# A list scheduler's cost table is lengthened, its integer additions move from VectorE to GpSimd, and the last output rows get buffers of their own

## The chip, the core and the metric

The kernel runs on one core of a Trainium2 chip. A core has a matrix engine (TensorE, "PE" in the profile; its weight loads are the row "PEld"), three engines that work elementwise (VectorE "DVE", ScalarE "ACT", GpSimd "POOL"), and a queue engine (SyncE "SP") that issues every transfer here. Each engine runs its own instruction list strictly in order and waits for the others by semaphores. The metric is device time in microseconds (us) of one execution; lower is better.

## The reference

Three layers follow each other: block-causal attention, a three-way maximum layer, and a squared-ReLU layer.

```python
scores = (1 / np.sqrt(64)) * np.matmul(q, k.transpose(0, 1, 3, 2))      # q, k, v: (4, 8, 576, 64)
scores = np.where(block_i >= block_j, scores, -1e9)                     # blocks of 64 rows
scores = scores - np.max(scores, axis=-1, keepdims=True)
attn = np.exp(scores)
attn = attn / (np.sum(attn, axis=-1, keepdims=True) + 1e-09)
x = np.matmul(attn, v).transpose(0, 2, 1, 3).reshape(2304, 512)
y = np.maximum(np.maximum(x @ w1, x @ w2), x @ w3) @ moe_w_out          # 512 -> 768 -> 512
h = np.maximum(y @ w_in, 0.0)                                           # 512 -> 2048
out = (h * h) @ w_out                                                   # 2048 -> 512
```

All is float32. The weights arrive as 64-bit numbers, which the kernel turns into float32 itself.

## The kernel before, in words

**Precision.** Most products are made of three matmuls: an operand is split into a rounded part and the rest ("h" and "l" tiles such as `w1h`, `w1l`, `xh`, `xl`), and low times high, high times low and high times high are added in PSUM.

**Stages.** In the first stage (0 to about 370 us) 16 pairs of heads go through attention (`attn_pair`) while the first dense layer (`mlp1`, PSUM tiles `l`) of the batches already done fills the gaps on PE. A pair runs through `step(i)` for i = 0 to 3 and `last_step`: score matmuls (`sc`), the masked corner written by a memset, the row maximum by a reduction on DVE (`nm`, negated), a small multiplication of `nm` by the scale 0.125, the exponential on ACT (`P`, which also applies the scale to the scores), transposes on PE (`tp`), copies of them on ACT (`ta`, `tb`), and the value matmuls (`av`). Pairs 0 to 3 use plain float32 scores; for pairs 4 to 15 `score_operands` rounds `qs`, `kh` and forms the rests. From about 370 to 510 us PE does the rest of `mlp1` alone, while DVE, ACT and POOL prepare the second layer's weights in eight rounds (`second_rows`, `first_rows`, tiles `wqf`, `wq`). From about 510 us the second dense pair runs as 3 passes of 8 blocks (`up`, `down`; PSUM tiles `ph`, `acc`), 24 blocks in all.

**Weight chunks.** `load_w_` turns one chunk of 128x512 64-bit numbers into float32 by integer work: two ACT instructions read the high and low halves, DVE shifts, DVE merges the sign (scalar_tensor_tensor), and an integer addition joins the two; then ACT rounds the high part and DVE forms the rest. There are 18 chunks of `w1`, 6 of `wo1` and 16 of `wo2` (tiles `wos`, started behind the 56th mark of attention) whose addition runs on DVE; the profile shows it as `CUSTOM_DVE_ANT_0`, the order as `ISA`. The 16 chunks of the second layer (`wi`) already add on GpSimd.

**What sets the order.** A list scheduler (`Plan`) records every operation with its operands, and `issue` then places them one by one: among all operations whose inputs are known it takes, for the engine that can begin earliest, the one with the lowest rank (attention 0, the first layer 1, `wo2` chunks 2). It reckons with the times of `duration`, with `SEM` (the delay from one engine to another), `LAP` (overlap of neighbours on one engine), with `transfer` for DMAs and with `HOLD` for the port that DVE and POOL share in its model. The order it finds is final: on the chip each engine follows it, whatever the real times are. Operations given to `nc.any` go to ACT or DVE as the plan finds it sooner.

**The last rows.** `down` ends a pass by copying six accumulators of 128x512 (1_0, 1_1, 1_2, 0_0, 0_1, 0_2 in this order) into `ob` tiles, by turns on ACT and DVE, and sending them out. All `ob` tiles share two buffers (tag `wraw`).

Of the kernel before, what the change touches and what calls it, by code (L numbers as in the profile page):

```python
# [43 lines left out]

CFG = dict(PD=-1, PE=1, A1=0, A2=0, WP=1, FC=(8, 16), WO=55, FI=0, LO2=0, HI2=0, Q2=0, RN=3, XL=2, HL=2, SO=0, TF=0, W_A=0.7, W_B=1.5, SPARE='hl..rhl..rhl..r..r..r', S=15, PB=3, QB=(2, 2, 3), BANKS=(3, 2, 1, 2), LO=0, HI=0, Q=0, EV=('a', 'a'), EV2=('a', 'a'), CB=2, PC=0, PM=1000, PX=-0.5, PO=0, HH='*', XH='*', N0='a', YS='a', HIS=0, RB=1, TB=(2, 1), KB=1, CT='a', LT='d', XA=4, XB=0)
W_A, W_B = CFG["W_A"], CFG["W_B"]
# [4 lines left out]
PB = CFG["PB"]  # L51
MASKED = -1000000000.0 / SCALE

# [115 lines left out]
class Plan:  # L169
# [56 lines left out]
    def issue(self):  # L226
# [11 lines left out]
        def offer(op):  # L238
            for e in op.engines:
                when = 0.0  # L240
                for d in op.deps:
                    when = max(when, d.end + (SEM[d.engine] if d.engine != e else 0))
                waiting[e][op.index] = when, shares_port(e, op)
# [4 lines left out]
        for _ in ops:  # L248
# [12 lines left out]
            op.engine = e  # L261
            length = duration(e, op)
            if e in held and waiting[e][i][1]:
# [26 lines left out]

HOLD = dict(dve=120, pool=60)


# [52 lines left out]
def fused_kernel(ctx: ExitStack, tc: tile.TileContext, z0, k0, qk, v, w123, wo1, win2, wo2, out):  # L346
# [6 lines left out]
    ident.tile.make()  # L353
    ident.tile.constant = True
    make_identity(tc.nc, ident.tile.real)
    dram = Pool(nc, dram)
# [17 lines left out]

    def load_w_(src, hi, lo, name, f=None, adder=nc.vector):
        spare = SPARE[len(chunks)] if len(chunks) < len(SPARE) else "."
# [25 lines left out]
        if not CFG["HIS"]:  # L402
            adder.tensor_tensor(out=fi, in0=fi, in1=qi, op=ALU.add)
        if hi is None:
# [44 lines left out]
    def score_operands(n):  # L449
# [3 lines left out]
        for h in range(2):  # L453
            raw = at.tile([128, 2, S], F32, tag="raw", bufs=CFG["RB"], name=f"raw{n}_{h}")
            nc.sync.dma_start(out=raw, in_=qk[n, :, h])
            qs, kh, kl = [at.tile([128, S], F32R, tag=t, bufs=m, name=f"{t}_{n}_{h}")
                          for t, m in zip(("qs", "kh", "kl"), CFG["QB"])]
            nc.scalar.copy(out=qs, in_=raw[:, 0])
            nc.scalar.copy(out=kh, in_=raw[:, 1])
            nc.vector.tensor_tensor(out=qs[64:128], in0=raw[64:128, 0], in1=qs[64:128].bitcast(F32), op=ALU.subtract)  # L460
            nc.vector.tensor_tensor(out=kl, in0=raw[:, 1], in1=kh.bitcast(F32), op=ALU.subtract)
            score.append([(qs, kh), (qs, kl)])
# [54 lines left out]
    def attn_pair(n, groups=(0, 1)):  # L517
# [29 lines left out]
        def step(i):  # L547
# [6 lines left out]
            if share:  # L554
                both = sc[0][:, :2 * N].rearrange("p (h k) -> p h k", h=2)
                sc = [both[:, h] for h in range(2)]
                P = [P[0][:, N * h:N * h + N] for h in range(2)]
            nm = small(f"nm{name}")
            sm = sums[i // 2][:, 2 * (i % 2):2 * (i % 2) + 2] if direct else small(f"sm{name}")
            for h in range(2):  # L560
                for c, (qp, kp) in enumerate(score[h]):
                    mm(sc[h][:, :N], qp[:, 128 * i - q0:128 * i - q0 + 128], kp[:, :N], start=c == 0,
                       stop=c == len(score[h]) - 1)
                if not share:
                    nc.vector.memset(sc[h][0:64, N - 64:N], MASKED)
                    nc.vector.tensor_reduce(out=nm[:, h:h + 1], in_=sc[h][:, :N], axis=AX.X, op=ALU.max, negate=True)
            if share:
                nc.vector.memset(both[0:64, :, N - 64:N], MASKED)
                nc.vector.tensor_reduce(out=nm, in_=both, axis=AX.X, op=ALU.max, negate=True)
            nc.vector.tensor_scalar(out=nm, in0=nm, scalar1=SCALE, scalar2=None, op0=ALU.mult)  # L570
            for h in range(2):
                act = nc.scalar.activation(out=P[h][:, :N], in_=sc[h][:, :N], func=AF.Exp, bias=nm[:, h:h + 1],
                                           scale=SCALE, accum_out=sm[:, h:h + 1])
            if not direct:
# [222 lines left out]
    def second_rows(q):  # L797
        f = forms_f[q] = w2p.tile([128, 8, 256], F32, tag="wqf", name=f"wqf{q}")
        load_w_(win2[q + NQ], None, None, f"wi_{q + NQ}", f[:, 0:2].rearrange("p i n -> p (i n)"), nc.gpsimd)

    def first_rows(q):
        f, w = forms_f[q], wq_tile(q)
        load_w_(win2[q], None, None, f"wi_{q}", f[:, 2:4].rearrange("p i n -> p (i n)"), nc.gpsimd)
        a21, a22, a11, a12, s1, s2, s3, s4 = [f[:, i] for i in range(8)]
# [132 lines left out]
    def down(p, q):  # L937

        for m, h in ((0, 0), (1, 1), (0, 1), (1, 0)):
            gh, gl = g_t.pop((p, q, m, h))  # L940
            hi, lo = wo_t[p, q + NQ * m]
            for s in range(TH // 128):
# [6 lines left out]
                if last:  # L949
                    ob = m1.tile([128, DM], F32, tag="wraw", bufs=2, name=f"ob{p}_{h}_{s}")  # L950
                    if s % 2:
                        nc.vector.tensor_copy(out=ob, in_=a)
                    else:
                        nc.scalar.copy(out=ob, in_=a)
                    t0 = 2 * TH * p + TH * h + 128 * s
                    nc.sync.dma_start(out=out[t0:t0 + 128, :], in_=ob)
                yield
# [77 lines left out]
```

## Time and profile before

| what | value |
|---|---|
| median of 3 runs | 896.17 us (895.51 to 896.87) |
| the profiled execution | 894.74 us |
| its span, first to last instruction | 893.0 us |
| PE busy, share of the span | 97% |
| DVE busy | 69% |
| ACT busy | 48% |
| POOL busy | 6% |
| share of PE in the chain that ended last | 88% |

The profiled execution is 1.4 us under the median, and its span 1.7 us under its own time. Busy times of PE are modelled at their ends, so a stretch in which PE shows no gap may still have room; gaps that are shown are real. The rows further down name an instruction by engine, operation, output<-input and shape; in square brackets stands the idle time of the engine just before it and what ended that.

### The profile page before, as it was taken

The page shows a single profiled execution, that of the slowest core. Times are in us where ns is not written, and L with a number is a line of the kernel's source. Part 1 is how long each engine was busy: PE and PEld are TensorE (multiplying, and loading weights), DVE is VectorE, ACT ScalarE, POOL GpSimd, SP SyncE. Part 2 cuts the span into 40 slices and gives each one's busy share as a digit, 9 for nine tenths or more (in the row PEclk, how much of TensorE's full clock was granted, in tenths as well). Part 3 has the DMA queues.
Part 4 walks back from the last instruction along what each step waited for, and adds up shares of the span by engine and source line. Part 5 has one row for each costly group of instructions (what it writes and reads, how often), then busy time and mean ns, then how long its engine had stood idle before and what let it go on. Part 6 is the DMA issues. An engine that isn't in the chain of part 4 may idle for free.

```text
span 893.0 us, 14824 instructions
## 1 busy us (share of the span) xinstructions
PE 868.1 (97%) x5464; PEld 778.7 (87%) x5464; DVE 617.1 (69%) x1454; ACT 424.6 (48%) x1023; POOL 50.9 (6%) x54
## 2 busy tenths in 40 slices
PE   6889999999999999999999999999999999999997
PEld 4667888998899978999999998898988889889885
DVE  5799888878798969846667774547755457545542
ACT  6798777777688578525546321113311114211111
POOL 0000000000000000015453300000000000000000
PEclk9999999999999999999999999999999999999999
DMA  9545432233356564435668485464755546564211
GB/s 299 184 157 165 154 123 86 85 103 125 101 175 232 164 209 156 158 125 216 232 253 314 134 293 192 159 229 165 277 218 188 202 152 232 204 226 164 78 64 71
DMA packets 51912, 157.73 MB, mean 177 GB/s; under 512 B 8576, under 2 KB 15744, under 8 KB 48256
## 3 DMA queue, kind: packets, MB, share of 16 engines
q1 hardware_dynamic: 51840, 156.78, 50.4%
q8 instruction: 43, 0.70, 0.3%
q14 instruction: 29, 0.24, 0.1%
HBM read 124.26 MB, written 32.51 MB: 176 GB/s over the span
## 4 chain that ended last, share of the span: by engine, by line
PE 88%; DVE 5%; DMA 3%; ACT 3%; issue 1%; SPq 0%; ACTq 0%; DVEq 0%
PE l L187 30%; PE acc L187 22%; PE ph_x L187 11%; PE ph_y L187 8%; PE av L187 6%; PE sc L187 5%; PE tp L187 4%; DMA raw<-in_qk 2%; PE sc_t L187 1%; DVE nm L187 1%; PE tp_t L187 1%; DMA raw_wo<-in_wo 1%; PE r L187 1%; DMA out<-ob 0%; DVE P L187 0%
## 5 line engine op out<-in xcount | busy, mean ns | idle before, releaser
L187 PE MATMUL acc<-woh,g 128*128 128x512 f32 x576 | 200.4, 396 | 0.0
L187 PE MATMUL l<-xh,w1l 128*128 128x256 f32 (+1 forms) x576 | 174.0, 302 | 0.0
L187 PE MATMUL l<-xl,w1h 128*128 128x256 f32 (+1 forms) x576 | 173.1, 300 | 0.0
L187 PE MATMUL l<-xh,w1h 128*128 128x256 f32 (+1 forms) x576 | 172.8, 300 | 0.0
L187 ACT CAST g<-c 128x384 fp32r<-128x384 f32 x96 | 49.2, 513 | 239.3 <-DVE c L187 239.2
L187 PEld LDWEIGHTS acc<-woh,g 128*128 128x128 f32 x576 | 108.1, 188 | 20.5
L187 PEld LDWEIGHTS l<-xh,w1l 128*128 128x128 f32 x576 | 109.7, 190 | 3.4 <-issue 1.7
L187 PE MATMUL acc<-wol,g 128*128 128x512 f32 x288 | 112.0, 389 | 0.0
L187 PEld LDWEIGHTS l<-xl,w1h 128*128 128x128 f32 x576 | 109.6, 190 | 2.7 <-issue 1.9
L187 PEld LDWEIGHTS l<-xh,w1h 128*128 128x128 f32 x576 | 109.6, 190 | 1.6 <-issue 1.0
L187 PE MATMUL ph_x<-t,wq 128*128 128x384 f32 x432 | 87.6, 338 | 0.0
L187 DVE TENSOR_TENSOR g<-c,g 128x384 fp32r<-128x384 f32 x96 | 53.2, 556 | 44.7 <-ACT g L187 44.3
L187 PEld LDWEIGHTS ph_x<-t,wq 128*128 128x128 f32 x432 | 77.4, 188 | 5.8
L187 ACT ACTIVATE P<-sc,nm 128x128 f32<-128x128 f32 (+3 forms) x128 | 67.2, 531 | 13.0 <-DVE nm L187 10.6
L187 DVE TENSOR_TENSOR run<-l,run 128x256 f32<-128x256 f32 (+1 forms) x96 | 43.5, 453 | 32.4 <-PE l L187 27.7
L187 PE MATMUL tp<-ident,P 128*128 128x128 f32 x320 | 51.0, 282 | 10.6 <-ACT P L187 10.2
L187 PEld LDWEIGHTS acc<-wol,g 128*128 128x128 f32 x288 | 54.2, 188 | 7.2
L187 PE MATMUL ph_y<-b,wq 128*128 128x384 f32 x288 | 58.4, 337 | 0.0
L187 PE MATMUL l<-hh,wo1l 128*128 128x256 f32 (+1 forms) x192 | 56.9, 299 | 1.4 <-DVE hh L187 1.3
L187 PE MATMUL l<-hl,wo1h 128*128 128x256 f32 (+1 forms) x192 | 57.1, 300 | 0.0
L187 PE MATMUL l<-hh,wo1h 128*128 128x256 f32 (+1 forms) x192 | 56.8, 298 | 0.0
L187 DVE TENSOR_REDUCE nm<-sc 128x2 f32<-128x256 f32 (+2 forms) x96 | 55.7, 591 | 0.8
(132 smaller groups left out, 1561.2 us busy)
## 6 DMA issues: line engine op xcount, KB each, us to landing
wq<-wq_d SPq DMA_DIRECT2D x20, 1792.0 KB, 8.2
wq_d<-wq SPq DMA_DIRECT2D x8, 1792.0 KB, 5.9
raw<-in_qk SPq DMA_DIRECT2D x24, 576.0 KB, 3.9
wol<-wo_d SPq DMA_DIRECT2D x48, 256.0 KB, 3.3
woh<-wo_d SPq DMA_DIRECT2D x48, 256.0 KB, 4.0
raw_wo<-in_wo SPq DMA_DIRECT2D x22, 512.0 KB, 3.6
raw_w<-in_w SPq DMA_DIRECT2D x18, 512.0 KB, 5.0
wo_d<-wos SPq DMA_DIRECT2D x16, 512.0 KB, 3.2
```

The lines of the kernel that those rows point to most:

```text
L187: return getattr(engine, op_name)(*map(value, args), **{k: value(x) for k, x in kw.items()})
```

## The change

- `issue` adds 500 ns to the moment from which PE may use what another engine made, and multiplies every DVE and ACT duration by 1.07 (`SLOW`).
- The integer addition of all chunks is recorded on GpSimd.
- `EV`: the copies `ta` go to `nc.any`, so the plan chooses ACT or DVE.
- For pairs 4 to 15 the scale 0.125 is applied when `qs` is rounded; the multiplication of `nm` is left out in their four steps (48 of 64).
- A small exponential on a new tile `warm` stands at the start.
- In the last pass the four last `ob` tiles get buffers that the first layer's weights had (`w1h0`, `w1l0`, `w1h1`, `w1l1`), chosen by (3h + s) modulo 4, and the last rows (0_2) are copied and sent in two halves.

```diff
@@ issue
-                    when = max(when, d.end + (SEM[d.engine] if d.engine != e else 0))
+                    when = max(when, d.end + ((SEM[d.engine] + (500 if e == 'pe' else 0)) if d.engine != e else 0))
...
-            length = duration(e, op)
+            length = duration(e, op) * SLOW[e]
...
+SLOW = dict(pe=1, dve=1.07, act=1.07, pool=1, sp=1)
@@ CFG
-EV=('a', 'a')
+EV=('*', '*')
@@ fused_kernel
+    warm = const.tile([128, 1], F32, name="warm")
+    tc.nc.vector.memset(warm, 0.0)
+    tc.nc.scalar.activation(out=warm, in_=warm, func=AF.Exp)
@@ load_w_
-            adder.tensor_tensor(out=fi, in0=fi, in1=qi, op=ALU.add)
+            nc.gpsimd.tensor_tensor(out=fi, in0=fi, in1=qi, op=ALU.add)
@@ score_operands
-            nc.scalar.copy(out=qs, in_=raw[:, 0])
+            nc.scalar.activation(out=qs, in_=raw[:, 0], func=AF.Copy, scale=SCALE)
...
-            nc.vector.tensor_tensor(out=qs[64:128], in0=raw[64:128, 0], in1=qs[64:128].bitcast(F32), op=ALU.subtract)
+            nc.vector.scalar_tensor_tensor(out=qs[64:128], in0=raw[64:128, 0], scalar=SCALE,
+                                           in1=qs[64:128].bitcast(F32), op0=ALU.mult, op1=ALU.subtract)
@@ step
+            scale = SCALE if sf else 1.0
...
-            nc.vector.tensor_scalar(out=nm, in0=nm, scalar1=SCALE, scalar2=None, op0=ALU.mult)
+            if sf:
+                nc.vector.tensor_scalar(out=nm, in0=nm, scalar1=SCALE, scalar2=None, op0=ALU.mult)
...
-                                           scale=SCALE, accum_out=sm[:, h:h + 1])
+                                           scale=scale, accum_out=sm[:, h:h + 1])
@@ down
-                    ob = m1.tile([128, DM], F32, tag="wraw", bufs=2, name=f"ob{p}_{h}_{s}")
-                    if s % 2:
-                        nc.vector.tensor_copy(out=ob, in_=a)
+                    if p + 1 == NPASS and (h, s) not in ((1, 0), (1, 1)):
+                        home = ("w1h0", "w1l0", "w1h1", "w1l1")[(3 * h + s) % 4]
+                        ob = w1p.tile([128, DM], F32, tag=home, name=f"ob{p}_{h}_{s}")
                     else:
-                        nc.scalar.copy(out=ob, in_=a)
+                        ob = m1.tile([128, DM], F32, tag="wraw", bufs=2, name=f"ob{p}_{h}_{s}")
                     t0 = 2 * TH * p + TH * h + 128 * s
-                    nc.sync.dma_start(out=out[t0:t0 + 128, :], in_=ob)
+                    parts = 2 if p + 1 == NPASS and (h, s) == (0, TH // 128 - 1) else 1
+                    for i in range(parts):
+                        n = slice(DM // parts * i, DM // parts * (i + 1))
+                        cp("d" if (s + i) % 2 else "a", out=ob[:, n], in_=a[:, n])
+                        nc.sync.dma_start(out=out[t0:t0 + 128, n], in_=ob[:, n])
```

The order changes nearly everywhere in the first stage. Three places matter for what follows. The first is the start of ACT's list: `P0_0_0` is the exponential of pair 0, step 0; `raw_w1_0_0` the first weight chunk. Before:

```order
L187 ACT_TABLE_LOAD
L187 ACTIVATE P0_0_0_127,sm0_0_128<-sc0_0_0_117,nm0_0_123 128x128 x2
L187 ACTIVATE raw_w1_0_0_83<-raw_w1_0_0_83 128x512
L187 COPY ta0_143<-tp0_0_0_138 128x2x128
L187 ACTIVATE P0_1_0_148,sm0_0_128<-sc0_1_0_120,nm0_1_135 128x256 x2
```

Now:

```order
L360 ACT_TABLE_LOAD
L360 ACTIVATE warm_61<-warm_61 128x1
L187 ACTIVATE raw_w1_0_0_86<-raw_w1_0_0_86 128x512
L187 ACTIVATE P0_0_0_138,sm0_0_139<-sc0_0_0_120,nm0_0_127 128x128 x2
L187 ACTIVATE P0_1_0_149,sm0_0_139<-sc0_1_0_122,nm0_1_135 128x256 x2
```

The table load and the small exponential stand ahead, the chunk has moved in front of the first exponential of the scores, and the copy of the first transposes has left the list.

The second is DVE around step 3 of pair 1: `sc1_3_0` and `sc1_3_1` are the scores of its two heads, `nm1_3` the maxima that its exponentials wait for, `w1l3` and `raw_w1_3_x` chunk work. Before:

```order
L187 ISA f_w1_3_0_594<-raw_w1_3_0_316,f_w1_3_0_594 128x1024
L187 SCALAR_TENSOR_TENSOR raw_w1_3_1_499<-raw_w1_3_1_499 128x512
L187 TENSOR_TENSOR xl0_1_677<-av0_1_586,xh0_1_663 128x320
L187 ISA raw_w1_3_1_499<-raw_w1_3_1_499 128x1024
L187 TENSOR_TENSOR w1l3_692<-f_w1_3_0_594,w1h3_675 128x512
L187 MEMSET sc1_3_0_564 64x64
L187 MEMSET sc1_3_1_650 64x64
L187 TENSOR_SCALAR raw_w1_3_2_579<-raw_w1_3_2_579 128x512
L187 TENSOR_REDUCE nm1_3_706<-sc1_3_0_564 128x1
L187 TENSOR_TENSOR w1l3_692<-raw_w1_3_1_499,w1h3_675 128x512
L187 TENSOR_REDUCE nm1_3_706<-sc1_3_1_650 128x1
```

Now:

```order
L187 MEMSET sc1_3_0_562 64x64
L187 SCALAR_TENSOR_TENSOR f_w1_3_0_551<-raw_w1_3_0_348,f_w1_3_0_551 128x512
L187 TENSOR_TENSOR run0_0_0_2_592<-l1_0_0_0_2_544,run0_0_0_1_534 128x256
L187 TENSOR_REDUCE nm1_3_596<-sc1_3_0_562 128x1
L187 TENSOR_TENSOR w1l2_526<-f_w1_2_2_488,w1h2_509 128x512
L187 TENSOR_SCALAR raw_w1_3_1_478<-raw_w1_3_1_478 128x512
L187 TENSOR_TENSOR w1l3_631<-f_w1_3_0_551,w1h3_617 128x512
L187 TENSOR_TENSOR av0_1_586<-av0_1_586,rs0_1_627 128x320
L187 SCALAR_TENSOR_TENSOR raw_w1_3_1_478<-raw_w1_3_1_478 128x512
L187 MEMSET sc1_3_1_629 64x64
L187 TENSOR_REDUCE nm1_t_652<-sc1_t0_637 128x1
L187 TENSOR_REDUCE nm1_3_596<-sc1_3_1_629 128x1
```

The two additions (`ISA`) are gone, and the first head's maximum has moved well ahead of the second's. On PE, 21 matmuls of `l` stood before between the scores `sc1_t0` of this pair and the transposes `tp1_3_0` of the exponentials; 35 stand there now.

The third is the end of SP's list, the transfers of the last rows (`ob2_h_s` for pass 2). Before:

```order
L187 DMA out_0<-ob2_1_0_9808 128x512
L187 DMA out_0<-ob2_1_1_9814 128x512
L187 DMA out_0<-ob2_1_2_9827 128x512
L187 DMA out_0<-ob2_0_0_9830 128x512
L187 DMA out_0<-ob2_0_1_9833 128x512
L187 DMA out_0<-ob2_0_2_9836 128x512
```

Now:

```order
L187 DMA out_0<-ob2_1_0_9763 128x512
L187 DMA out_0<-ob2_1_1_9768 128x512
L187 DMA out_0<-ob2_1_2_9774 128x512
L187 DMA out_0<-ob2_0_0_9780 128x512
L187 DMA out_0<-ob2_0_2_9788 128x256 x2
L187 DMA out_0<-ob2_0_1_9793 128x512
```

The rows 0_1 have moved behind 0_2: their buffer, number 1 of the four, is also that of 1_2. DVE's list ends in the same way, with the second half of 0_2 and then 0_1.

Farther on, the preparation of the second layer's weights has moved back against PE: the first round begins behind the 1548th matmul of `l` instead of the 1476th, and the last round's casts stand behind the start of the third stage as they did before, but now with a second round close ahead of them.

## Rows read from the trace of the kernel before

**Rows 1.** Page, part 1: busy us (share), instructions.
```profile
PE 868.1 (97%) x5464; PEld 778.7 (87%) x5464; DVE 617.1 (69%) x1454; ACT 424.6 (48%) x1023; POOL 50.9 (6%) x54
```

**Rows 2.** Stretches: start:end length, busy by engine (instructions), granted clock, DMA share, GB/s.
```profile
20.00:29.00 9.00, 5.64 (x24) 3.99 (x23) 8.86 (x25) 6.06 (x18) 0.00 (x0) 0.88 0.95 321
...
57.00:62.00 5.00, 1.71 (x15) 1.34 (x15) 5.00 (x14) 5.00 (x13) 0.00 (x0) 1.00 0.14 58
62.00:70.00 8.00, 8.00 (x40) 4.77 (x40) 7.83 (x21) 6.10 (x17) 0.00 (x0) 0.79 0.57 189
70.00:310.00 240.00, 239.12 (x1792) 212.56 (x1789) 210.32 (x645) 183.33 (x502) 0.00 (x0) 1.00 0.43 136
310.00:346.00 36.00, 33.05 (x239) 28.42 (x239) 25.84 (x66) 25.27 (x65) 0.00 (x0) 1.00 0.57 186
...
510.40:883.00 372.60, 372.60 (x1859) 335.45 (x1858) 211.47 (x384) 77.65 (x145) 1.49 (x3) 1.00 0.51 185
```

**Rows 3.** PE's waits over the run: total us, times, longest.
```profile
PE tp L187 <- ACT P L187: 10.2, 4, 3.3
```

**Rows 4.** Weight loads' waits, 70 to 310 us.
```profile
PEld av L187 <- issue: 3.5, 14, 0.3
...
PEld av L187 <- ACT t L187: 1.1, 3, 0.8
```

**Rows 5.** Timeline, the start: us, duration, instruction [idle before].
```profile
6.24 1.28 ACT L187 ACT_TABLE_LOAD   x1 [6.24 <-DVE nm L187]
...
20.15 3.14 PEld L187 LDWEIGHTS sc<-zk 128*128 128x128 f32 x16 [0.45 <-DMA zk<-in_z]
...
27.10 0.37 ACT L187 ACTIVATE P<-sc,nm 128x128 f32<-128x128 f32 x1 [2.89 <-DVE nm L187]
...
27.61 0.68 PE L187 MATMUL tp<-ident,P 128*128 128x128 f32 x2 [3.27 <-ACT P L187]
```

**Rows 6.** The first chunk's transfer, issued at 2.59: us to landing.
```profile
DMA to landing us min/median/max: 5.4/5.4/5.4
```

**Rows 7.** Timeline, step 3 of pair 1.
```profile
60.47 0.72 ACT L187 ACTIVATE P<-sc,nm 128x512 f32<-128x512 f32 x1
...
61.33 0.66 PE L187 MATMUL tp<-ident,P 128*128 128x128 f32 x4 [3.29 <-ACT P L187]
```

**Rows 8.** Timeline, one of two waits between 310 and 346 us.
```profile
318.72 0.65 ACT L187 ACTIVATE raw_wo<-raw_wo 128x512 int32<-128x512 uint32 x1 [2.35 <-DMA raw_wo<-in_wo]
...
320.54 0.41 PE L187 MATMUL l<-hh,wo1l 128*128 128x320 f32 x1 [1.32 <-DVE hh L187]
```

**Rows 9.** Groups over the run by shape: count, busy us, mean ns, idle before.
```profile
L187 DVE CUSTOM_DVE_ANT_0 f_wo<-raw_wo,f_wo 128x1024 uint16<-128x1024 uint16 x22 | 15.0, 680 | 0.5
...
L187 DVE TENSOR_SCALAR nm<-nm 128x2 f32<-128x2 f32 x64 | 10.0, 157 | 0.1
...
L187 POOL TENSOR_TENSOR wqf<-wqf,raw_wi 128x512 int32<-128x512 int32 x16 | 22.3, 1395 | 459.2 <-DVE wqf L187 434.4 <-issue 17.0 <-ACT wqf L187 5.2
```

**Rows 10.** The same DVE group beside POOL (392 to 480 us).
```profile
L187 DVE TENSOR_TENSOR hl<-run,hh 128x256 fp32r<-128x256 f32 x6 | 4.8, 801 | 2.3 <-ACT hh L187 2.3
```

**Rows 11.** And without POOL (200 to 312 us).
```profile
L187 DVE TENSOR_TENSOR hl<-run,hh 128x256 fp32r<-128x256 f32 x6 | 2.5, 416 | 0.1
```

**Rows 12.** Timeline, DVE: the last second-layer weight tile before.
```profile
520.45 1.22 DVE L187 TENSOR_TENSOR wq<-wqf,wq 128x1024 fp32r<-128x1024 f32 x1
```

**Rows 13.** Timeline, the end.
```profile
883.06 0.59 ACT L187 COPY ob<-acc 128x512 f32<-128x512 f32 x1 [5.07 <-PE acc L187]
...
885.81 0.59 ACT L187 COPY ob<-acc 128x512 f32<-128x512 f32 x1 [2.16 <-PE acc L187]
886.03 0.39 PE L187 MATMUL acc<-woh,g 128*128 128x512 f32 x1
...
888.71 0.69 DVE L187 COPY ob<-acc 128x512 f32<-128x512 f32 x1 [4.28 <-DMA out<-ob]
889.37 0.58 ACT L187 COPY ob<-acc 128x512 f32<-128x512 f32 x1 [2.15 <-DMA out<-ob]
```

## What the change should do to the time

> **What bounds the kernel now.** I read the page's first part, then the stretches, then PE's waits, then the timeline at each place where PE stands still. PE is busy for 868.1 of 893.0 us [rows 1], so no other engine's time counts by itself: only time in which PE has nothing to do. The stretches say where that is [rows 2]. From 510.4 to 883 PE fills all of its 372.6 us; the two dense layers there can gain nothing. From 70 to 310 it lacks only 0.9 of 240 us. The gaps are in four places. The start: 20 to 29 us has 5.64 busy of 9.00. One hole: 57 to 62 has 1.71 of 5.00. Two smaller ones: 310 to 346 has 33.05 of 36.00. And the end, where the last matmul starts at 886.03 and runs 0.39, but the span ends at 893.0 [rows 13]. Together the first three lack 3.4 + 3.3 + 3.0 = 9.7 us, and the end takes 6.6.
>
> The waits name the cause of the largest: transposes waited 10.2 us in 4 cases for exponentials on ACT [rows 3]. The exponential of the third pair began at 27.10, when ACT had idled 2.89 us for the maxima on DVE, and PE had then idled 3.27 [rows 5]; that of pair 1, step 3 began at 60.47, PE idle for 3.29 [rows 7]. DVE meanwhile was full: 8.86 of 9.00 and 5.00 of 5.00 [rows 2]. So the reader is to see one pattern: DVE, in order, has weight-chunk work in front of the maxima, while PE's list has the transposes in front of matmuls that it could run. The two places after 310 have another cause: ACT stood 2.35 us at a chunk whose transfer had not landed, what was behind it came late, and PE waited 1.32 [rows 8]; a second wait there is of the same kind.
>
> **The change part by part.** All gains are worked out against the profiled execution, 894.74 us with a span of 893.0; the median of the runs is 1.4 above it, and I carry the same difference over.
>
> *DVE's load.* 40 additions at 0.680 [rows 9] leave DVE: 27.2 us. 48 of the 64 small multiplications at 0.157 [rows 9] go: 7.5. Thirteen copies `ta` come to it; at 0.69 for a copy of 512 columns from PSUM [rows 13] that is 9 at most, and since most are half as wide I take 6. The scale inside the `qs` instructions I price at 0: the same elements pass the same engines once, and these pairs come after 70 us, where ACT is busy for 183 of 240 us [rows 2]. That is -29 us of DVE, in the first stage and a little behind it, where PE does not wait for DVE except in the gaps above. So this part is worth something only there.
>
> *What the additions cost on GpSimd.* One takes 1.395 us [rows 9], 0.7 longer than on DVE, in a chain that feeds `w1` tiles. Behind it wait ACT's rounding of the chunk, DVE's rest, and on SP the next chunk's transfer (its buffer is now freed by POOL), with the operand transfers of later pairs queued behind that. Also, DVE slows down beside POOL: the same group `hl` takes 801 ns between 392 and 480 us, where POOL works, and 416 where it does not [rows 10, 11]. 40 additions are 55.8 us of POOL. From below: no instruction of DVE meets one, 0. From above: each addition holds DVE for its whole length, 55.8 us. In between, `hl` lost 6 x 0.385 = 2.3 us, and it is one of some six groups so placed beside POOL's 50.9 us [rows 1]; I take 12 us as an estimate. DVE's relief is then 17 us, with ends of 29 and -27.
>
> The Trainium skill speaks against this part. "SBUF — State Buffer", section "Who interferes with whom", says that DVE and GpSimd share a port pair which is locked for a whole instruction, so the later one blocks fully if DVE reads two SBUF operands or runs in a two-port mode; "GPSIMD Engine Reference", section "Engine selection", advises against two-input elementwise work there. The `hl` rows agree that something blocks [rows 10, 11]. By the rule at its worst DVE is 27 us busier, and the time goes the second rival's way; by the rows it is 17 us freer.
>
> *The start.* The table load of 1.28 us at 6.24 [rows 5] goes ahead of everything. But ACT's list now has the first chunk in front of the first exponential, and that chunk lands at 2.59 + 5.4 = 8.0 [rows 6]; with 0.65 for such a read [rows 8] the exponential starts about 8.6, not 7.5. This part alone loses about 1 us, and neither sign matters much: the third pair's scores can't begin before 20.15, when their operands land [rows 5], and the transfers' order ahead of that is unchanged. What counts is the third pair's exponential at 27.10. In front of its maxima DVE loses four additions (2.7 us), and two chunk instructions of about 0.7 each have moved behind them; two narrow `ta` copies come in, 0.4 each as an estimate under the 0.69 above: -3.3 us. ACT's list is next late: with its start at 8.6 instead of 7.5 and its own chunk work it arrives near 25. I take -2.0, ends 0 and -3.3.
>
> *Step 3 of pair 1.* Ahead of its maxima two additions are gone (1.4 us), the first maximum is earlier, and 14 more matmuls of `l` stand on PE before the transposes; at 240 / 1,792 = 0.13 us for a matmul [rows 2] these are 1.9 us. 3.29 - 1.4 - 1.9 = 0.0. I take -2.4, since the `l` matmuls themselves may now wait for evictions; ends 0 and -3.3.
>
> *The clock behind that hole.* Between 62 and 70 us the granted clock was 0.79 [rows 2], that is 1.2 GHz for a part of it, after PE had idled; 8.0 x 0.21 = 1.7 us lost. If the hole goes, this goes: -1.5, ends 0 and -1.7.
>
> *310 to 346 us.* The cause is a late transfer, and neither the 500 ns nor the 7% touches how the plan reckons transfers. The 0.5 us of margin can shorten two waits of about 1.3 each: -1.0, ends 0 and -2.6.
>
> *The 500 ns between 70 and 310.* Weight loads there wait mostly for nothing that the profile shows (3.5 us in 14 cases of at most 0.3), and 1.1 us for ACT in three [rows 4]. The plan's new margin can win only the second sort: -0.5, ends 0 and -3.
>
> *The end.* Each `ob` buffer is free again 885.81 - 883.65 = 2.16 us after its copy ended, and 3.0 us pass between the end of the last copy (889.37 + 0.58) and the end [rows 13]. Now 1_2 has its own buffer: its copy can follow its accumulator at 884.43 (883.06 plus two groups of matmuls at 0.69) and ends at 885.02. The half copies of 0_2 start at 886.5 on ACT and 886.9 on DVE. But 0_1 shares its buffer with 1_2: free at 885.02 + 2.16 = 887.2, DVE reaches it at 887.3, ends 0.69 later at 888.0, and the span ends at 891.0. That is -1.9, with ends of -1.4 and -2.2. Without the shared buffer it would be -3.
>
> *New waits.* A new order of some 3,000 instructions puts other waits in place of the old ones. The trace can't show them. From below 0; from above as much as stands still now in the three places, 9.7 us, less the part that only the operands' landing sets, 8. I take +1.5, nearest to 70 to 310, where the present order lost 0.9 us in 240.
>
> *The second layer's weights.* Their preparation begins 72 matmuls of `l` later against PE, at the same 0.13 us about 10 us. The last tile was ready at 521.7 [rows 12] and is first needed in the fourth of 24 blocks of 15.5 us each, over two blocks behind 510.4: not before 541. 20 us of cover; I cost it at 0. The DVE work of one more round now lies in a stage where DVE has 211 of 373 us busy [rows 2].
>
> Sum: -2.0 - 2.4 - 1.5 - 1.0 - 0.5 - 1.9 + 1.5 = **-7.8 us**. 894.74 - 7.8 = 886.9 for a profiled execution; 896.17 - 7.8 = **888.4** for the median.
>
> **The rivals.** *First: the waits move and do not vanish.* The plan's errors about transfers and about DVE stay, so PE stands elsewhere for as long; the new order then wins only the end, and 0.3 us by chance: 896.17 - 1.9 + 0.3 = 894.6. For it: two of the gaps come from transfers, and the order is fixed whatever the chip does. Against it: between 70 and 310 us an order from the same planner lost next to nothing, and the hole at 57 has a cause that the change removes twice over.
>
> *Second: GpSimd blocks DVE, and the time is longer.* The place is the first 70 us, where 14 of the 40 additions run (an estimate from the order) and DVE has no slack. It decides from 29 / 40 = 0.7 us of blocking per addition: above that DVE is busier than before. At the full 1.395 those 14 cost DVE 14 x 0.7 = 10 us more; the third pair's maxima would come some 3 us later than now and step 3 of pair 1 another 4 or so, of which 5 reach PE: 896.17 - 1.9 + 5 = 899.3. For it: the rows beside POOL. Against it: they show half of that, beside an instruction which does meet POOL.
>
> *Third: more than forecast.* All good ends together are -16.1, 880.1. *Fourth: the weights of the second layer come too late*; it needs the preparation to slip by 20 us and not 10, and would cost the excess, say 5: 899.
>
> **How the numbers follow.** Forecast 0.66; more than that (below 881.5) 0.12; the first rival 0.14; the second 0.06; the fourth 0.02. A measurement here can tell 0.2%, 1.8 us, from no change: same is 894.4 to 898.0. Forecast and third rival are faster, and of the first about one part in six: 0.80; same 0.12; slower 0.08. The range takes the forecast with its ends and the first rival's middle: 881.5 to 895.0; below it stays 0.12, above it 0.1.
>
> **What would show it.** In the changed profile: the third pair's transposes near 25.5 us, not 27.6; no idle of over 1 us before the transposes of pair 1, step 3, and a full clock after it; PE idle between 310 and 346 still there, near 2 us; between 70 and 310 under 3 us; the additions on POOL at 1.4 to 2 us and DVE's `hl` and `w1l` slower beside them; the last copy on DVE, waiting for a transfer, 3 us ahead of the end; PE without a gap from 510 us on, shifted. The forecast is wrong if PE's waits in the first 350 us sum up to as much as now, or if the second stage no longer runs PE without gaps.

## The result and the profile after

The changed kernel takes 887.69 us (median; 885.7 to 888.7) beside 895.88 for the kernel before: a ratio of 0.9904, 95% interval 0.9884 to 0.9924, or 8.2 us less between the medians. The forecast was 888.4. The profiled execution took 888.7 us with a span of 886.9, beside 894.74 and 893.0 before. It is the longest of its four and lies 1.0 us above their median, the one of the kernel before 1.1 under its own: the two traces read below differ by 6.0 us, not 8.2.

The page's first part, and then the stretches with the columns of [rows 2]; the last three stretches are new:

```profile
PE 864.2 (97%) x5464; PEld 777.7 (88%) x5464; DVE 601.1 (68%) x1376; ACT 424.9 (48%) x1016; POOL 104.0 (12%) x94
```

```profile
20.00:29.00 9.00, 6.71 (x34) 4.70 (x34) 8.84 (x25) 6.72 (x24) 2.60 (x2) 1.00 0.86 289
57.00:62.00 5.00, 5.00 (x29) 3.40 (x28) 4.92 (x17) 4.34 (x12) 1.30 (x1) 1.00 0.43 109
62.00:70.00 8.00, 8.00 (x61) 5.45 (x60) 6.67 (x16) 6.83 (x18) 2.81 (x2) 1.00 0.63 222
70.00:310.00 240.00, 237.83 (x1788) 214.59 (x1788) 194.83 (x567) 178.20 (x486) 19.84 (x14) 0.99 0.39 125
...
310.00:346.00 36.00, 36.00 (x275) 30.73 (x274) 29.74 (x89) 29.81 (x82) 3.90 (x3) 1.00 0.52 180
...
107.50:111.00 3.50, 3.50 (x19) 3.50 (x19) 0.77 (x2) 0.59 (x2) 0.00 (x0) 0.51 0.51 128
...
495.00:530.00 35.00, 32.30 (x169) 29.71 (x169) 23.12 (x40) 12.59 (x22) 12.46 (x12) 0.95 0.68 245
520.50:524.00 3.50, 3.50 (x11) 2.93 (x11) 2.88 (x5) 0.51 (x1) 2.74 (x3) 0.51 0.41 138
```

Beside [rows 2], the hole at 57 is full (5.00 for 1.71) and has the full clock behind it, 310 to 346 is full (36.00 for 33.05), and the start is fuller. Worse are 70 to 310 us (2.17 us lacking for 0.88) and a new place at 495 to 530. PE's waits over the run (total us, times, longest) show which waits went and which came; they answer [rows 3]:

```profile
PE sc L187 <- DMA zk<-in_k: 7.5, 3, 3.5
PE tp L187 <- ACT P L187: 2.8, 3, 1.6
PE ph_x L187 <- ACT p L187: 2.7, 1, 2.7
PE l L187 <- DVE wo1l L187: 2.1, 2, 1.7
PE l L187 <- DVE run L187: 0.9, 1, 0.9
```

The transposes wait 2.8 us for exponentials and no longer 10.2. The scores wait longer for the transfers of their operands, all in the first 21 us; before, that row was:

```profile
PE sc L187 <- DMA zk<-in_k: 3.5, 1, 3.5
```

New are waits for `wo1l` (98 and 104 us), one for `run` (368), and one in the last stage, where there was none. The first `ph_x` of that stage begins at 501.71; before it began at 510.28. So the kernel was 8.6 us ahead there and handed in only 6.1 of span. What it lost stands in the timeline (us, duration, engine, instruction, [idle before]):

```profile
516.67 0.65 ACT L187 ACTIVATE raw_wi<-raw_wi 128x512 int32<-128x512 uint32 x1 [4.05 <-DMA raw_wi<-in_win]
...
518.60 0.50 ACT L187 CAST g<-c 128x384 fp32r<-128x384 f32 x1
519.00 0.47 ACT L187 COPY p<-ph_x 128x384 f32<-128x384 f32 x1
...
519.52 1.50 PE L187 MATMUL ph_x<-t,wq 128*128 128x384 f32 x6 [2.70 <-ACT p L187]
```

ACT stood 4.05 us at a chunk of the second layer whose transfer had not landed; behind it in ACT's list stood the copy `p` that PE needed. The transfers of this last round were issued late, and took longer (KB each, median us to landing; in the second fence the first row is for 505 to 520 us, the second for 400 to 480):

```profile
506.26 2.02 SPq L187 DMA_DIRECT2D raw_wi<-in_win  x2
```

```profile
raw_wi<-in_win SPq DMA_DIRECT2D x2, 512.0 KB, 10.2
raw_wi<-in_win SPq DMA_DIRECT2D x12, 512.0 KB, 4.6
```

Behind PE's wait the granted clock fell to half (0.51 from 520.5 to 524): another 3.5 x 0.49 = 1.7 us. With the 2.70 us of waiting that makes 4.4.

The start answers [rows 5]; the first exponential, the third pair's scores, its first exponential and its transposes:

```profile
8.14 0.35 ACT L187 ACTIVATE P<-sc,nm 128x128 f32<-128x128 f32 x1
...
20.63 2.86 PE L187 MATMUL sc<-zk 128*128 128x128 f32 x16 [1.96 <-DMA zk<-in_k]
...
25.26 0.37 ACT L187 ACTIVATE P<-sc,nm 128x128 f32<-128x128 f32 x1 [2.25 <-DVE nm L187]
...
25.77 0.68 PE L187 MATMUL tp<-ident,P 128*128 128x128 f32 x2 [1.63 <-ACT P L187]
```

The granted clock in the first 70 us changed as well; before, then after:

```profile
0.00:70.00 70.00, 55.50 (x333) 38.65 (x333) 54.62 (x144) 54.21 (x142) 0.70 (x6) 0.93 0.66 218
0.00:70.00 70.00, 57.85 (x374) 39.89 (x375) 57.88 (x148) 56.11 (x146) 21.20 (x21) 1.00 0.70 230
```

Before, 70 x 0.07 = 4.9 us went to a lower clock: at 62 to 70 us, and also at 18 to 21.5 and 28.4 to 31.8, where it was half. The changed kernel had the full clock in all three places.

The end answers [rows 13]:

```profile
880.14 1.27 ACT L187 COPY ob<-acc 128x512 f32<-128x512 f32 x2 [0.77 <-PE acc L187]
...
881.76 0.39 PE L187 MATMUL acc<-woh,g 128*128 128x512 f32 x1
882.18 0.37 ACT L187 COPY ob<-acc 128x256 f32<-128x256 f32 x1 [0.77 <-PE acc L187]
882.59 1.05 DVE L187 COPY ob<-acc 128x256 f32<-128x256 f32 x2 [2.43 <-ACT ob L187]
```

The last matmul ends at 882.15, the span 4.75 us later; before it was 6.6. DVE's last row holds two copies without a gap: the rows 0_1 stood in its list behind the half of 0_2, and waited for no transfer.

### The profile page after: what moved, and what is told of

Read it like the earlier page. It is cut to its first block, busy times and chain, and to the rows that moved or that the text cites. A ratio compares the mean times of both kernels' runs of the same rounds, so it can differ in the third digit from the quotient of the medians.

```text
span 886.9 us, 14852 instructions
## 1 busy us (share of the span) xinstructions
PE 864.2 (97%) x5464; PEld 777.7 (88%) x5464; DVE 601.1 (68%) x1376; ACT 424.9 (48%) x1016; POOL 104.0 (12%) x94
## 4 chain that ended last, share of the span: by engine, by line
PE 92%; DVE 2%; DMA 2%; ACT 2%; issue 0%; POOL 0%; SPq 0%; ACTq 0%; POOLq 0%; DVEq 0%
PE l L187 34%; PE acc L187 22%; PE ph_x L187 11%; PE ph_y L187 8%; PE av L187 5%; PE sc L187 5%; PE tp L187 4%; PE sc_t L187 2%; DMA raw_wi<-in_win 1%; PE tp_t L187 1%; DMA raw_wo<-in_wo 1%; DMA zk<-in_k 1%; PE r L187 0%; ACT P L187 0%; DVE f_wo L187 0%
## 5 line engine op out<-in xcount | busy, mean ns | idle before, releaser
L187 POOL TENSOR_TENSOR f_wo<-f_wo,raw_wo 128x512 int32<-128x512 int32 x22 | 29.8, 1357 | 276.5 <-DVE sm L187 180.3
```

The source lines that it names most:

```text
L187: return getattr(engine, op_name)(*map(value, args), **{k: value(x) for k, x in kw.items()})
```

## The experiments

Two theories stood at first. ORDER: the plan's longer reckoning put other work in front of what comes late. RELIEF: VectorE, with less to do, was simply earlier. A third, BLOCKING, is the second rival's mechanism and could take RELIEF back: GpSimd's additions hold VectorE up. The first two runs hold every engine's list fixed and move the additions alone, in the old list and in the new; `to` is the engine that gets the instruction, while the plan still reckons with `e`.

### The old list, additions on GpSimd (a_before_pool)

```diff
@@ issue (before)
+            to = 'pool' if e == 'dve' and op.kw.get('op') == ALU.add and op.kw['out'].area.shape == (128, 512) and not any(x.psum for x in op.views()) else e
-            self.tc.keep_in_program_order(self.call(self.real[e], alias(e, op.name), op.args, op.kw))
+            self.tc.keep_in_program_order(self.call(self.real[to], alias(e, op.name), op.args, op.kw))
```

> The kernel before, with every engine's list kept word for word, except that the 40 integer additions stand in GpSimd's list instead of VectorE's. No other part of the change. Theory ORDER (the plan's longer reckoning made the gain of the first stage): PE's list is the old one, so the waits move little; only what the additions took ahead of the two late maxima goes, 1.4 us at pair 1 step 3 and at most 2.7 us at the start: 0 to -2 us of the time. Theory RELIEF (VectorE's freed time made it): both waits shrink by these amounts and the half clock behind the hole at 57 us goes: -4 to -6 us. Theory BLOCKING (the port they share takes the relief back): VectorE's busy time falls by less than 27.2 us, by 0 at the worst, and the time is the same or up to 5 us longer; the forecast's own estimate of 12 us of blocking would leave VectorE at 602 us of 617.

Measured: 910.15 us beside 895.64, ratio 1.0170 (1.0151 to 1.0188). RELIEF and ORDER both fall for this list; it is BLOCKING, and three times as dear as its worst estimate. The page's engine row, two DVE groups (count, busy us, mean ns), and the hole, now near 62 us:

```profile
PE 872.9 (96%) x5464; PEld 780.8 (86%) x5464; DVE 615.4 (68%) x1414; ACT 425.4 (47%) x1023; POOL 108.2 (12%) x94
```

```profile
L187 DVE TENSOR_TENSOR w1l<-f_w,w1h 128x512 fp32r<-128x512 f32 x12 | 11.3, 946 | 0.8 <-ACT w1h L187 0.8
...
L187 DVE TENSOR_SCALAR f_w<-f_w 128x512 int32<-128x512 int32 x12 | 7.9, 666 | 0.0
```

```profile
60.39 1.29 DVE L187 TENSOR_TENSOR w1l<-f_w,w1h 128x512 fp32r<-128x512 f32 x1 [0.40 <-ACT w1h L187]
...
64.82 3.22 POOL L187 TENSOR_TENSOR raw_w<-raw_w 128x512 int32<-128x512 int32 x1 [3.69 <-DVE nm L187]
...
65.81 0.47 PE L187 MATMUL tp<-ident,P 128*128 128x128 f32 x1 [3.51 <-ACT P L187]
```

In the kernel before, the same two DVE groups took 680 and 412 ns, not 946 and 666. DVE lost 27.2 us of additions and yet is busy for 615.4 us, not 589.9: 25.5 us, or 0.64 per addition, went to instructions that take longer beside POOL. POOL is held up too: one addition took 3.22 us, where one at 59.82 took 1.31 (spans on POOL are rough). The Trainium skill ("SBUF — State Buffer", "Who interferes with whom") says that of two such instructions the one that comes second is blocked fully, whichever it is; both rows agree. The second rival named 0.7 us as the point from which the time rises. It rose at 0.64, by 14.5 us, with DVE busy for 1.7 us less than before: DVE's load, which is all that the rival priced, does not account for it. That each chunk's longer chain, in a list which does not reckon with it, delays what stands behind is the likely rest; no run here separates it from the blocking.

### The new list, additions on VectorE (b_after_dve)

The same edit in the changed kernel, from `pool` to `dve`, for the 40 additions that the change moved.

> The changed kernel, with every engine's list kept word for word, except that the 40 integer additions stand in VectorE's list at the place where the plan put them for GpSimd. ORDER: the margins cover it, so the time stays within 1.5 us of the changed kernel (about 888 to 889). RELIEF: waits of PE for exponentials and for first-layer weights come back, 3 to 6 us over the changed kernel (891 to 894). BLOCKING: as fast or faster than the changed kernel, since no instruction of VectorE is held up any more; VectorE busy less than 601 + 27 us by as much as the blocking took.

Measured: 886.01 us, ratio 0.9898 (0.9880 to 0.9916), not to be told from the changed kernel's 0.9904. DVE is 11.9 us busier (613.0), and the hole stays closed:

```profile
57.00:62.00 5.00, 5.00 (x35) 3.82 (x35) 4.43 (x12) 4.38 (x11) 0.00 (x0) 1.00 0.32 92
```

So RELIEF falls: once the list is made, where the additions run is worth nothing that can be measured. In the new list BLOCKING costs 601.1 - (613.0 - 27.3) = 15.4 us of DVE (27.3 is what the 40 additions take there), 0.39 per addition. It lies mostly where PE does not wait for it: PE's waits for `wo1l` are 1.1 us here and 2.1 in the changed kernel.

### The plan's two numbers alone (c_plan, then h_plan_wo46)

c_plan is the kernel before with only the 500 ns and the 1.07.

> The kernel before with the plan's two numbers alone (500 ns on what PE takes from others, 1.07 on VectorE's and ScalarE's durations); additions stay on VectorE, no new buffers, no new copies. ORDER: most of the first stage's gain without the additions, 4 to 6 us less than before (890 to 892), and no idle over 1 us of PE before the transposes of pair 1 step 3. RELIEF: within 2 us of before, with PE waits of some 8 us left in the first 350 us.

Measured: 896.79 us, ratio 1.0013 (0.9998 to 1.0029): no gain. The trace shows where it went. First the third pair's first exponential and the wait at the hole, then the end of the first stage, then the stretch after 310:

```profile
25.15 0.37 ACT L187 ACTIVATE P<-sc,nm 128x128 f32<-128x128 f32 x1 [1.80 <-DVE nm L187]
...
58.29 0.66 PE L187 MATMUL tp<-ident,P 128*128 128x128 f32 x4 [2.30 <-ACT P L187]
```

```profile
402.31 0.62 ACT L187 CAST wos<-f_wo 128x512 fp32r<-128x512 f32 x1 [3.43 <-DMA wo_d<-wos]
402.83 0.42 ACT L187 COPY run<-l 128x320 f32<-128x320 f32 x1
...
403.30 0.63 PE L187 MATMUL l<-xh,w1l 128*128 128x320 f32 x1 [9.32 <-ACT run L187]
```

```profile
310.00:346.00 36.00, 36.00 (x282) 32.11 (x281) 31.78 (x102) 28.61 (x79) 0.00 (x0) 1.00 0.66 207
```

The margins close 310 to 346 by themselves, and the third pair's exponential begins at 25.15 for 27.10, with all additions still on DVE. They do not close the hole at 57, where 2.30 us of 3.29 are left. And they push the `wo2` chunks back (the last rounding `wos` is at 402.31; before it was at 380.8). Their last ones stand at the end of the first planned part, each waiting for the transfer of the one before (there is one `wos` buffer), ahead of a `run` that PE needs: 9.32 us. The kernel calls `issue` once for this part and once for the rest, so nothing of the rest can pass them. h_plan_wo46 has the same margins and lets the chunks begin earlier (`WO=55` becomes `WO=46`).

> The kernel before with the plan's two numbers alone, as c_plan, but the weight chunks wo2 may begin behind the 47th mark of attention instead of the 56th. In c_plan PE stood 9.3 us at 394 us behind ACT's list, where the last wo2 chunks, waiting for each other's transfers, stood ahead of a copy of run. Theory ORDER: the margins do win the first 370 us (c_plan's PE excess there is 21 us beside before's 31), and c_plan only lost it again at that one place: 9.3 us of wait and about 2 us at half clock behind it. With the chunks earlier: 885 to 888. Theory RELIEF (without the additions on GpSimd the plan finds nothing): the chunks' wait moves into attention, 892 to 897.

Measured: 890.47, ratio 0.9940 (0.9918 to 0.9962). The wait of 9.3 us is gone and 5.4 us of gain appear. That is 2.5 less than ORDER wanted and outside RELIEF's range too; the transposes still wait 6.1 us in three cases, the hole among them. The earlier chunks without the margins were not run; on the mended kernel below they win nothing (k_mended46), so that the 5.4 us come from the margins is likely, not shown.

### All but the two numbers (d_after_noplan)

```diff
@@ issue (after)
-                    when = max(when, d.end + ((SEM[d.engine] + (500 if e == 'pe' else 0)) if d.engine != e else 0))
+                    when = max(when, d.end + (SEM[d.engine] if d.engine != e else 0))
...
-            length = duration(e, op) * SLOW[e]
+            length = duration(e, op)
```

> The changed kernel without the plan's two numbers (no 500 ns, no 1.07); additions on GpSimd, copies by the plan's choice, scaled queries, warm exponential and new buffers stay. ORDER: PE waits in the first 370 us again as before, +6 to +9 us on the changed kernel (894 to 897). RELIEF: within 2 us of the changed kernel (886 to 890).

Measured: 890.65, ratio 0.9951 (0.9932 to 0.9970). Between the two expectations: the margins are worth some 3 us within the whole change by the medians, 4 by the ratios. The trace is of an execution of 893.64, 3.0 us above the median of its twelve. An instruction of ACT ahead of the third pair's exponential, the third pair's transposes, those of pair 1, step 3, the next wait, and two stretches:

```profile
25.42 0.62 ACT L187 CAST w1h<-f_w 128x512 fp32r<-128x512 f32 x1 [2.33 <-POOL f_w L187]
...
27.68 0.68 PE L187 MATMUL tp<-ident,P 128*128 128x128 f32 x2 [2.96 <-ACT P L187]
...
58.27 0.60 PE L187 MATMUL tp<-ident,P 128*128 128x128 f32 x4
...
61.79 0.44 PE L187 MATMUL tp_t<-ident,P_t 128*128 128x128 f32 x2 [0.93 <-ACT P_t L187]
```

```profile
57.00:62.00 5.00, 4.08 (x29) 2.93 (x29) 3.79 (x10) 4.88 (x12) 2.17 (x2) 1.00 0.26 78
310.00:346.00 36.00, 35.28 (x255) 30.23 (x255) 25.10 (x62) 26.84 (x68) 5.67 (x4) 1.00 0.48 166
```

So the two halves do different things. The margins bring the third pair's exponential forward. Without them ACT's list has the rounding of two chunks in front of it, each waiting for an addition on GpSimd: it begins at 27.18, and PE waits 2.96 us, nearly the 3.27 of the kernel before, though the additions have left DVE. The other half removes the wait of pair 1, step 3: its transposes begin without one here, and the 0.92 us that PE lacks between 57 and 62 belong to another wait, for `P_t`. From 310 to 346 either half does most of it.

In this other half the plan reckons an addition at some 1.3 us on POOL instead of 0.7 on DVE. With b_after_dve this points to the *reckoning* and not the engine. The step that the scaled queries save can't be what helps at the hole, for pair 1 keeps its multiplication of `nm`. But the copies `ta` and the new start belong to this half too, and which part of it acts at the hole was not separated.

### The last rows alone (e_tail)

The kernel before with the change in `down` only.

> The kernel before with the own buffers and the halves for the last rows alone; the lists of the first stage are those of before. The forecast's term for the end: -1.9 us, ends -1.4 and -2.2, so 894.0 beside 895.9; the span ends some 4.7 us behind PE's last matmul instead of 6.5. The rival term (no collision of buffers counts): -3 us.

Measured: 893.82, ratio 0.9979 (0.9965 to 0.9993): -1.9 us. The last matmul ends at 886.92, the span at 891.4, 4.5 us later.

### Mending the two weak places (f_after_wi_homes)

```diff
@@ issue (after)
-                op.end, free[e] = queue + 400, t + 60
+                late = 6000 if any(n in x.tile.kw['name'] for x in op.views() for n in ('raw_wi_3', 'raw_wi_11')) else 0
+                op.end, free[e] = queue + 400 + late, t + 60
@@ down (after)
-                        home = ("w1h0", "w1l0", "w1h1", "w1l1")[(3 * h + s) % 4]
+                        home = ("w1h0", "w1l0", "w1h1", "w1l1")[h + s]
```

> The changed kernel with two mendings. (1) The plan reckons the transfers of the second layer's last round (chunks 3 and 11) 6 us longer, so that ACT's reads of them stand behind the copy p of the second block and the casts g, not ahead. If the wait of 2.7 us at 516 and the half clock behind it come from ACT standing at that transfer: both go, -4.4 us. If they come from the later preparation as such: the wait moves to another place behind 510 us and the time stays. (2) The last rows 1_2 and 0_1 no longer share a buffer: the forecast's -3 us instead of -1.9, so -1.1. Both: 882.2 beside 887.7; the span ends some 3.7 us behind PE's last matmul.

Measured: 881.31, ratio 0.9847 (0.9821 to 0.9873): 6.4 us under the changed kernel by the medians, 5.1 by the ratios. The last stage's start, ACT there, and the end:

```profile
495.00:530.00 35.00, 35.00 (x194) 32.98 (x194) 26.95 (x46) 13.06 (x24) 11.87 (x12) 1.00 0.74 274
```

```profile
514.17 0.48 ACT L187 COPY p<-ph_x 128x384 f32<-128x384 f32 x1 [1.85 <-PE ph_x L187]
...
517.16 0.67 ACT L187 ACTIVATE wqf<-raw_wi 128x512 f32<-128x512 f32 x1
...
876.86 0.39 PE L187 MATMUL acc<-woh,g 128*128 128x512 f32 x1
...
877.69 0.42 DVE L187 COPY ob<-acc 128x256 f32<-128x256 f32 x1 [0.39 <-ACT ob L187]
```

The chunk is read at 517.16, as late as ever, but `p` now stands ahead of it: PE does not wait, and the clock stays full. It was the place in ACT's list, not the late preparation: the last weight tile is ready even later here, at 537.6 (533.2 in the changed kernel), and PE waits for neither. The end is 4.05 us behind the last matmul (4.75 with the shared buffer): 0.7 us, not 1.1. So 4.4 + 0.7 = 5.1 us are read from the traces. Both mendings were in one run, and only the traces tell them apart.

### Other parts, on the mended kernel (i_best2, j_nowarm, i_best, k_mended46, k_noqs46)

i_best2 moves the additions to DVE in the mended list:

> f_after_wi_homes with its lists kept, only the 40 additions emitted into VectorE's list at the places that the plan chose for GpSimd. BLOCKING (GpSimd's additions cost VectorE about 0.4 us each through the shared port, and their longer chain makes w1 and wo1 tiles late): 1 to 2 us faster, 879.5 to 880.5. RELIEF: 2 us or more slower than 881.3.

Measured: 882.28, ratio 0.9851 (0.9835 to 0.9868), the same as 0.9847. So neither expectation is met: here too the place of the additions makes no difference.

j_nowarm leaves out the small exponential:

> f_after_wi_homes (881.3) without the small exponential at the start; all other rows of the lists are the same. The table load of 1.28 us then comes where ACT meets its first real activation. In f_after_wi_homes the first chunk stands in front of the first exponential and is read when its transfer lands, near 7.6 us. If the load waits there behind it, the exponential starts 1.3 us later (9.4 and not 8.1) and the start loses up to 1.3 us. If the load goes while ACT waits for the transfer, or if the third pair's operands set the start's length anyway, nothing: within 1 us of 881.3.

Measured: 883.46, ratio 0.9870 (0.9855 to 0.9885). That is 2.1 us above the mended kernel's median, more than the 1 us expected, but the intervals overlap. ACT's first rows:

```profile
0.73 1.28 ACT L187 ACT_TABLE_LOAD   x1 [0.73 <-PEq L1039]
7.57 0.66 ACT L187 ACTIVATE raw_w<-raw_w 128x512 f32<-128x512 f32 x1 [5.56 <-DMA raw_w<-in_w]
8.13 0.35 ACT L187 ACTIVATE P<-sc,nm 128x128 f32<-128x128 f32 x1
```

The load goes at 0.73 in any case, while ACT waits for the chunk; the changed kernel's first exponential began at 8.14. The trace gives the small exponential nothing to win; the 2.1 us stay unexplained.

i_best joins b_after_dve's placing, the two mendings and `WO=46`:

> As f_after_wi_homes, but with the additions emitted into VectorE's list at the places that the plan chose for GpSimd (as b_after_dve), and wo2 chunks from the 47th mark on, so that the preparation of the second layer has more cover. b_after_dve was 1.7 us faster than the changed kernel: if that adds to the two mendings (-5.5): 880.5. If the plan's list for the earlier wo2 chunks makes new waits in attention: 882 to 886.

Measured: 883.42, ratio 0.9864 (0.9837 to 0.9890), in the second of the two ranges and no better than the mended kernel. k_mended46 and k_noqs46 test the scaled queries:

> f_after_wi_homes with the wo2 chunks from the 47th mark on instead of the 56th, additions on GpSimd: the base for k_noqs46. The preparation of the second layer then has 10 us more of cover; the mended list has no wait left there, so nothing is gained behind 370 us: 880 to 883.

> k_mended46 with the scale 0.125 back in the exponential and the 48 small multiplications of nm back on VectorE (48 x 0.157 = 7.5 us). The forecast priced this part at 0 where PE does not wait for VectorE: within 1.5 us of k_mended46. RELIEF: the multiplication stands in the chain from the maxima to the exponential and the waits of transposes for exponentials grow in the first 350 us: 2 to 4 us slower.

Measured: 882.14, ratio 0.9858 (0.9843 to 0.9873), within its range, and 884.85, ratio 0.9882 (0.9867 to 0.9897), in RELIEF's. The intervals still overlap a little: 2 to 3 us for the scaled queries are likely, not shown. The transposes' waits for exponentials are 3.5 and 3.8 us, so RELIEF's own mechanism is not what is seen. The copies `ta` were not tried alone.

## Why the prediction came out

The number held, 888.4 for 887.69, and in part by luck: gains that were priced too low or not at all made up for a loss that was priced at nothing. By its own last sentence the forecast also fell on one point, for the second stage no longer runs PE without gaps. The terms, read from the two traces:

- **The start** (-2.0): the third pair's transposes began at 25.77, 1.84 us earlier than in [rows 5], but not for the cause given. The prediction had four additions less in front of the maxima; d_after_noplan has them off DVE and its exponential begins at 27.18; c_plan has them on DVE and it begins at 25.15, as in the changed kernel (25.26). It was the margins. The step inside it on ACT was roughly right: the chunk landed at 7.57, not 8.0, and the first exponential began at 8.14, 0.6 late and not 1. That the operands set the scores held as well: they began at 20.63, on a transfer. No term stood for the granted clock here: of the 4.9 us that it cost before in the first 70, some 3.2 lay ahead of the hole. They are gone in this trace, but not for sure in every execution: f_after_wi_homes had 0.84 again from 20 to 29 us.
- **The hole and the clock behind it** (-2.4 and -1.5): 3.29 us and 1.7, near the good ends. The cause given was wrong in part. "Two additions are gone" explains little: with them back on DVE in the new list the hole stayed shut, and without them in the old list, where blocking lengthened other work of DVE, PE still waited 3.51 us. It was the order, and of the change's two halves the one without the margins.
- **310 to 346 us** (-1.0): all 2.95 us went. The step that failed is "the 0.5 us of margin can shorten two waits". c_plan shows the margins alone removing waits longer than themselves; a margin changes which instruction stands in the gap. They are not the only way, for d_after_noplan has 35.28 of 36.00 without them.
- **The 500 ns from 70 to 310** (-0.5) **and new waits** (+1.5): idle there rose by 1.3 us, and 1.7 went to a half clock at 107.5, behind the wait for `wo1l`. About half of that wait is the chain through GpSimd that the prediction named: with the additions on DVE the waits for `wo1l` are 1.1 us instead of 2.1. With `run` at 368 (0.9) the new waits up to the last stage come to some 4 us, where these two terms together gave +1.0; the upper end was +8.
- **The second layer's weights** (0): the step that failed most. The cover of 20 us was counted to the first use of the last tile, and PE never waited for that tile. The price came from ACT's list: the chunk's first read stood ahead of the copy `p`, and its transfer took 10 us where those between 400 and 480 us took 4.6. The prediction did ask elsewhere what is queued behind a waiting instruction, but not for the step that moved here. It cost 4.4 us; f_after_wi_homes wins them back. The slip was mis-sized too: 10 us against PE is near what the first round shows (its first read was 116.8 us ahead of the stage's first `ph_x` before and is 104.1 now), but the last tile was ready 31.5 us behind the stage's first `ph_x` (533.2 - 501.7) and before 11.4 (521.7 - 510.3), which is 20 us.
- **The end** (-1.9): -1.8 in the trace, -1.9 in e_tail. The shared buffer cost 0.7, not 1.1.
- **DVE's load** (-17 us): 617.1 to 601.1, so -16; blocking 15.4 for the estimated 12. The additions took 1.36 to 1.39 us on POOL, under the 1.4 to 2 expected. That this relief is worth something only in the gaps was right, and too kind: with 11.9 us of it taken back, b_after_dve is no slower.

The sum: up to the last stage the traces differ by 8.6 us where the terms gave 5.9; there 4.4 were lost; the end gave 1.8. 8.6 - 4.4 + 1.8 = 6.0, as the spans differ by 6.1. Of the 8.6, PE's idle time fell from 18.3 to 15.2 us, which is 3.1, and the lower clock cost 4.9 before and 1.7 after, which is 3.2. Some 2 us can't be read as idle time or clock; they lie in stretches that both traces show as full.

Two sums among the prediction's rivals do not hold: the fourth rival's excess of 5 us on top of the forecast gives 893.4, not 899, and the first rival adds 0.3 us that its sentence says are won.

## What to carry to other kernels

With a fixed order, an estimate must follow a moved step into each engine's list and ask what stands behind it there, above all when it begins with a transfer: 20 us of cover for its result did not help, because a transfer of 10 us held up a neighbour. Moving work to an idle engine has to be judged together with the list that it is planned in: the same 40 additions cost 14.5 us in a list made without them and nothing in one made for them. Where one late transfer costs, lengthening that one transfer in the plan can be enough: f_after_wi_homes closed the last stage's gap so, with the margins of the changed kernel kept; against margins everywhere it was not tried.

## What the runs showed of the hardware

- A small instruction of DVE can lose the whole length of an integer addition on GpSimd beside it: the additions of a constant to 128x5 elements (`sm`) took 1.04, 0.60, 0.17 and 1.30 us in the changed kernel, a mean of 776 ns, and 167 ns in the mean with the integer additions on DVE.
- The same wait did not always cost the clock: 1.7 us for `wo1l` near 104 us was followed by half clock in the changed kernel, while in f_after_wi_homes the like wait left the clock at 1.00; there it was 20 to 29 us that showed 0.84. So a stretch at half clock, 1.7 us each in these traces, can come and go between two runs, and two traces should be compared with it set apart.
